# An attention block gated by a mish MLP: products of y in pairs, activations in half places, another order, sums of y in the tail

## The chip, the cores and the metric

The kernel runs on one core of one Trainium2 chip. The metric is device time in microseconds of one execution. Three runs of the kernel before took 3404.28, 3404.55 and 3408.29 us, the median is 3404.55 us.

## The reference

The input x has 2048 rows of 1024 columns, all in float32. There are 32 heads of 32 columns, and the MLP has 3584 hidden columns.

```python
xn = _layernorm(x)
qkv = xn @ wqkv                                   # 1024 -> 3 * 1024
scores = einsum("bhqd,bhkd->bhqk", q, k) * 32 ** -0.5
o = einsum("bhqk,bhkd->bhqd", softmax(scores), v)
s = o @ wo
h = xn @ w1 + b1                                  # 1024 -> 3584
act = h * tanh(softplus(h))                       # mish
g = silu(act @ w2)                                # 3584 -> 1024
out = x + s * g
```

## The kernel before, in words

**Numbers.** Every float32 factor is split in a high part of type fp32r and a low part (what the high part leaves), and a product is three products of such parts (`THREE`). The high parts are mostly copied by ScalarE (`copy`, L276), the low parts are made by VectorE or GpSimd (POOL) as original minus high (`low`, L284). Every matmul writes up to 512 columns into one of eight PSUM banks.

**Stages.** Rows are cut in 16 tiles of 128 and in four chunks of 512. First x is loaded, normalised and turned by TensorE tile by tile, beside the first pass of v (`ln_a` ... `ln_c`, `v_group`, L325); four blocks of W1 are split meanwhile (`w1_first`). Then come two more passes of v, and the projection to q and k (L725), each with splits of further weights in its shadow.

Then comes the planned stage, with five streams of matmuls: s (scores with rows on partitions, only for the maximum of each row, L803; VectorE takes the maxima, L809), t (scores again, transposed, with the maximum subtracted in the product, L890; ScalarE makes p = exp from them, L273), h (hidden columns of the MLP, L1049), y (activations by w2, L1190) and, last, op (the output projection of the first chunk, L1317). The p tiles (2048 columns, six places) are multiplied by v (pv, narrow matmuls, L938) in groups of four, and added to z by POOL (L919) for the sum of the softmax, which a narrow product with ones takes at the end of a head (zp, L974). VectorE adds the pv of a head to o (L950).

**y by seven products.** w2 is multiplied with Strassen's seven products instead of eight. A unit is two hidden blocks of 128 (56 units: 14 in each of the four chunks). `mish` makes four activations of a unit, x, y, z and w, as high and low; x, y and z have 512 columns and w 256; `YSEQ` names the seven products. For each unit and product TensorE makes two sums of three matmuls, each in a bank of its own, and VectorE subtracts each from one of 14 accumulators `yacc` (L1213); the first unit of a chunk is copied by ScalarE. When a chunk is through, seven sums on POOL (`y_sums`, L1226) combine the seven products, and four blocks of 512 KB are stored to `ys`.

**Who sets the order.** The class `Plan` works out, while the program is built, when each engine would be free, and writes the instructions in that order: an operation (`Op`) has an engine, a duration, operations that it needs, and places that it takes and gives in rings: `b` (the eight banks, all), `s`, `t` and `d` (at most so many of the banks for s, for t, and for h and y), `p` (p tiles), `act` and `aw` (activations), `w1`, `w2`. A matmul of a stream has a due time: t by its tile of p, s by the same less `LEAD` tiles, h and y by their unit, y with offsets `Y0` and `Y1`. `run` takes the engine that is free first, gives it the ready operation with the lowest key, and looks again. For VectorE the key is the time at which an operation was ready, less its `urgent` value (`U_MX` for the maxima, `U_Y` for the adds of y).

**q and k of a head** lie in `qstack` and `kstack` (three of each); a head's kstack is free again after the last t of the head, and then holds the head three further on (`stack_load`).

**The tail** (`new_o` to the end) multiplies chunks 1 to 3 of o by wo. Each chunk's eight parts of o are loaded, split into `ohl` or `xo` by `split_o`, and 24 matmuls make half of one of the 16 tiles of the output. `start` loads x and y of a tile, ScalarE takes Silu of y, and `end` multiplies (L1420), adds x (L1421) and stores (L1425). Six places hold x and six y.

Of the kernel before, what the change touches and what calls it, by code (L numbers as in the profile page):

```python
# [26 lines left out]
W1_0, W1_V = 4, 21  # L27
# [7 lines left out]
GROUPS = (4, 4, 4, 4)  # L35

LEAD, LATE = 14, 3.0

PS, ACTS, W1S, W2S, Y0, Y1 = 6, 4, 3, 3, 1.2, 0.14
# [6 lines left out]
S_B, T_B, D_B = 3, 2, 5  # L46

U_MX, U_Y = -3.0, 4.0
# [24 lines left out]
class Op:  # L73


    def __init__(self, eng, took, need=(), emit=None, take=(), give=(), key=None, col=False, late=0.0,
                 bytes_=0, then=None, first=False, both=False, urgent=0.0):
        self.eng, self.took, self.need, self.emit = eng, took, need, emit
        self.take, self.give, self.key, self.col, self.late = take, give, key, col, late
        self.bytes, self.then, self.first, self.both, self.urgent = bytes_, then, first, both, urgent  # L80
        self.end = None


class Plan:
# [94 lines left out]
    def run(self, streams):  # L179
        self.streams = [[s, None] for s in streams]  # L180
        while True:
# [5 lines left out]
            for e in sorted(left, key=self.at.get):  # L187
                now, best, soon = self.at[e], None, None
# [26 lines left out]
                later = [self.at[x] for x in left if self.at[x] > now] + ([soon] if soon is not None else [])  # L215
                if later:
                    self.at[e] = min(later)
                    break
            else:
                raise AssertionError("nothing can go on")  # L220
# [3 lines left out]
def body(ctx: ExitStack, tc: tile.TileContext, x, wqk, wv, wo, w1, b1, w2, out):  # L224
# [21 lines left out]
    ys = [dram.tile([P, 4, D], F32, name=f"ys{i}") for i in range(NC)]  # L246
# [113 lines left out]
    def x_load(t):  # L360
        xt = vp.tile([P, D], F32, tag="x", name=f"x{t}", bufs=5)
        nc.sync.dma_start(xt, x[t * P:(t + 1) * P, :])
# [4 lines left out]
    def split_w(w, raw, job=False):  # L367
        for half in range(2):
# [5 lines left out]
    def w1_first(n, step):  # L374
        t, g = xc[2 + n // 2], n % 2
        raw = first_w1[n // 2][:, g]
        w = t[:, 1, 4 * g:4 * g + 4].rearrange("p k n -> p (k n)") \
# [3 lines left out]
        elif step == 1:  # L381
            split_w(w, raw, True)
# [25 lines left out]
    def ln_b(t):  # L408
        mv, var, rs = stat.pop(t)
        tmps[t] = tmp = vp.tile([P, 1], F32, tag="tmp", name=f"tmp{t}", bufs=3)  # L410
        nc.vector.scalar_tensor_tensor(tmp, rs, var, rs, op0=ALU.mult, op1=ALU.mult)
# [5 lines left out]
    def ln_x(t):  # L417
        tmp, rs = tmps.pop(t)
        act(xts[t], xts[t], AF.Identity, bias=tmp, scale=rs)
# [40 lines left out]
    for t in range(2, NT + 2):  # L460
# [17 lines left out]
        for step, n in enumerate((t - 2, t - 3, t - 5)):  # L478
            if 0 <= n < W1_0:
# [293 lines left out]
    for name, n in (("b", 8), ("s", S_B), ("t", T_B), ("d", D_B), ("o", 1), ("p", PS), ("z", 1), ("e", 1), ("n", 1), ("r", 1), ("on", 1),  # L773
                    ("act", ACTS), ("aw", 1), ("g", 1), ("w1", W1S), ("w2", W2S), ("xc", 1), ("v", 1), ("mx", 2), ("nm", 2), ("hl", 2),
# [101 lines left out]
    def t_stream():  # L876
        pts = {}
        for T in range(NS):
# [29 lines left out]
            if kt:  # L908
# [20 lines left out]
    def product(T, pts, size):  # L929
# [23 lines left out]
        if kt == NT - 1:  # L953

            need.append(adds[T])
# [5 lines left out]
        if kt == NT - 1:  # L961
            norm(h, got[h], adds[T])
# [3 lines left out]
    def norm(h, product_, sum_):  # L966
# [4 lines left out]
        def z_mm(at):  # L971
            t["z"] = bank(at, f"zp{h}")
            for c in range(4):
                nc.tensor.matmul(t["z"][c * DH:(c + 1) * DH, :], ones, zs[h][:, c * 512:(c + 1) * 512],  # L974
                                 start=True, stop=True)
# [23 lines left out]
        a = own = op("PE", 1.0, need=[sum_], emit=z_mm, take=["d", "b"], give=["z"], col=True, late=LATE)  # L999
# [19 lines left out]
    def w2_op(m, need=()):  # L1019
        def emit(at):  # L1020
            w2t[m] = mlp.tile([P, 2, 512], F32R, tag=f"w2{at['w2']}", name=f"w2_{m}")
            move(w2t[m], w2s[m // 7 % U][:, m % 7])
# [40 lines left out]
    def mish(n, made, t):  # L1063
# [9 lines left out]
        def a2(at):  # L1073
            t["q"] = t["h"]
# [5 lines left out]
        def a3(at):  # L1080
            t["r"] = mlp.tile([P, 512], F32, tag="r0", name=f"r{n}")
            act(t["r"], t["q"], AF.Ln, bias=one)

        def d3(at):
            t["n"] = mlp.tile([P, 512], F32, tag="n0", name=f"n{n}")
            nc.vector.scalar_tensor_tensor(t["n"], t["e"], 2.0, t["h"], op0=ALU.add, op1=ALU.mult)

        def a4(at):
            act(t["r"], t["r"], AF.Exp, scale=-1.0)

        def d4(at):
            nc.vector.scalar_tensor_tensor(t["q"], t["q"], 1.0, t["r"], op0=ALU.add, op1=ALU.mult)

        def d5(at):
            nc.vector.scalar_tensor_tensor(t["q"], t["q"], 2.0, t["r"], op0=ALU.subtract, op1=ALU.mult)

        def d6(at):
            nc.vector.tensor_tensor(t["h"], t["h"], t["n"], ALU.mult)

        def hi(kind, r, src):  # L1100
            def emit(at):
                ring = "aw" if kind == "w" else "act"
                if (n // 2, kind) not in acts:
                    w = 256 if kind == "w" else 512
                    acts[n // 2, kind] = mlp.tile([P, 2, w], F32R, tag=f"{ring}{at[ring]}", name=f"a{kind}{n // 2}")
                copy(acts[n // 2, kind][:, 0, r], src()[:, r])
            return emit

        def lo(kind, r, src, eng=None):
            def emit(at):  # L1110
                a = acts[n // 2, kind]
                low(eng or nc.vector, a[:, 1, r], src()[:, r], a[:, 0, r])
            return emit

        L, R, LR = slice(0, 256), slice(256, 512), slice(0, 512)
# [23 lines left out]
        o3 = op("DVE", 0.69, need=[o2], emit=d3, take=["n"])  # L1139
        p2 = op("ACT", 0.69, need=[o3], emit=a2, give=["e"])  # L1140
        p3 = op("ACT", 0.68, need=[p2], emit=a3, take=["r"])
# [3 lines left out]
        o6 = op("DVE", 0.69, need=[o5], emit=d6, give=["n"])  # L1145
# [354 lines left out]
```

## Time and profile before

| what | us |
|---|---|
| median of three runs | 3404.55 |
| the profiled execution's own time | 3404.78 |
| its span, first to last instruction | 3403.0 |
| x, first pass of v | 0 to 83 |
| passes two and three of v | 83 to 213.5 |
| q and k | 213.5 to 583 |
| planned stage | 583 to 3199.4 |
| its end: last y, op of chunk 0 | 3199.4 to 3273 |
| tail: op of chunks 1 to 3 | 3273 to 3403 |

Engines are PE (TensorE's matmuls), PEld (its weight loads, which run beside them), DVE (VectorE), ACT (ScalarE), POOL (GpSimd) and SP (which issues nearly all transfers). A group's row gives line, engine, operation, output and inputs by the program's names, sizes and count, then the busy time and the mean of one in ns, then the idle time ahead of it and what ended it. A row of waits says who waited for whom: total, count and longest. The chain goes back from the last instruction to what released each step.

### The profile page before, as it was taken

The numbers are of one execution on the slowest core, as the hardware profiler recorded it, in microseconds if no ns is written. First come the engines' busy times: TensorE is split into PE (matmuls) and PEld (weight loads), VectorE is DVE, ScalarE is ACT, GpSimd is POOL, SyncE is SP. The second block draws the span as 40 slices with busy tenths as digits, with TensorE's granted clock in tenths as the row PEclk, the third lists the DMA queues.
The fourth block names the chain that finished last, engine by engine and source line by source line (L and its number), as shares of the span: only waits on it lengthen the run. The fifth ranks groups of instructions, "written<-read, shape, count | busy, mean of one in ns | idle before, by whom it ended". The sixth has DMA issues, their size and how long they took to land.

```text
span 3403.0 us, 48050 instructions
## 1 busy us (share of the span) xinstructions
PE 3350.0 (98%) x17107; PEld 2444.7 (72%) x17107; DVE 2683.6 (79%) x4462; ACT 2039.2 (60%) x3394; POOL 2727.3 (80%) x923
## 2 busy tenths in 40 slices
PE   8999999999999999999999999999999999999999
PEld 8898887767766766667777676666776666677587
DVE  6024446999999998889999988889999889896753
ACT  6112222766766667767776677667776776677621
POOL 3547662998898989999989899989988999899910
PEclk9999999999999999999999999999999999999999
DMA  8989997544555465545455564445556555546582
GB/s 285 339 307 370 369 367 243 143 137 138 154 150 148 144 192 180 149 131 153 141 157 157 182 186 137 140 141 148 149 164 198 163 149 158 150 146 193 171 306 85
DMA packets 257633, 639.87 MB, mean 188 GB/s; under 512 B 90266, under 2 KB 99482, under 8 KB 248730
## 3 DMA queue, kind: packets, MB, share of 16 engines
q1 hardware_dynamic: 254948, 628.42, 58.7%
q10 hardware_dynamic: 2448, 8.39, 0.6%
q8 instruction: 136, 2.23, 0.3%
q14 instruction: 101, 0.83, 0.1%
HBM read 474.97 MB, written 160.69 MB: 187 GB/s over the span
## 4 chain that ended last, share of the span: by engine, by line
PE 84%; DVE 7%; DMA 3%; POOL 2%; issue 2%; ACT 1%; SPq 1%; ACTq 0%; DVEq 0%; POOLq 0%
PE h L1049 16%; PE y L1190 13%; PE pv L938 13%; PE s L803 12%; PE t L890 12%; PE qk L725 8%; PE op L1317 4%; PE v L325 4%; DVE mx L809 2%; DMA kstack<-ks 1%; POOL z L919 1%; DVE yacc L1213 1%; ACT p L273 1%; PE zp L974 1%; POOL pw L284 1%
## 5 line engine op out<-in xcount | busy, mean ns | idle before, releaser
L919 POOL TENSOR_TENSOR z<-z,p 128x2048 f32<-128x2048 f32 x448 | 2066.5, 4613 | 75.0 <-ACT p L273 50.6
L273 ACT ACTIVATE p<-t,zero 128x512 f32<-128x512 f32 x2048 | 1366.5, 689 | 455.8 <-PE t L890 436.0
L809 DVE TENSOR_REDUCE mx<-s 128x1 f32<-128x512 f32 x1984 | 1283.4, 682 | 65.9 <-PE s L803 63.4
L890 PE MATMUL t<-qstack,kstack 128*128 128x512 f32 x2048 | 791.3, 394 | 1.8 <-ACT p L273 0.9
L803 PE MATMUL s<-kstack,qstack 128*128 128x512 f32 x1984 | 755.6, 397 | 14.8 <-DMA kstack<-ks 7.5
L1049 PE MATMUL h<-xr,w 128*128 128x512 f32 x2016 | 676.6, 390 | 1.4 <-DVE aw L284 0.6
L1213 DVE TENSOR_TENSOR yacc<-yacc,y 128x512 f32<-128x512 f32 x728 | 492.6, 680 | 36.8 <-PE y L1190 33.3
L803 PEld LDWEIGHTS s<-kstack,qstack 128*128 128x128 f32 x1984 | 366.8, 188 | 160.8 <-issue 26.8
L890 PEld LDWEIGHTS t<-qstack,kstack 128*128 128x128 f32 x2048 | 382.0, 188 | 126.5 <-issue 28.5
L938 PE MATMUL pv<-p,v 128*32 128x512 f32 x4096 | 466.0, 595 | 1.0 <-ACT p L273 0.6
L1049 PEld LDWEIGHTS h<-xr,w 128*128 128x128 f32 x2016 | 377.6, 188 | 84.1 <-DVE aw L284 2.1
L725 PE MATMUL qk<-xc,qkw 128*128 128x512 f32 x1536 | 351.3, 389 | 0.3
L725 PEld LDWEIGHTS qk<-xc,qkw 128*128 128x128 f32 x1536 | 288.0, 188 | 60.8 <-DVE mx L607 1.2
L938 PEld LDWEIGHTS pv<-p,v 128*32 128x32 f32 x4096 | 119.9, 109 | 276.4 <-issue 247.6
L919 POOL TENSOR_TENSOR z<-p,p 128x2048 f32<-128x2048 f32 x32 | 147.8, 4620 | 159.5 <-PE zp L974 107.1
L1190 PE MATMUL y<-w,az 128*128 128x512 f32 x672 | 232.1, 395 | 4.7 <-POOL az L284 1.7
L1190 PE MATMUL y<-w,ay 128*128 128x512 f32 x672 | 227.2, 391 | 3.4 <-ACT ay L276 1.4
L1190 PE MATMUL y<-w,ax 128*128 128x512 f32 x672 | 225.1, 391 | 2.2 <-DVE ax L284 0.7
L1049 PE MATMUL h<-xc,w 128*128 128x512 f32 x672 | 225.7, 391 | 0.0
L950 DVE TENSOR_TENSOR o<-o,pv 128x512 f32<-128x512 f32 x96 | 65.9, 687 | 117.0 <-PE pv L938 112.9
L1190 PEld LDWEIGHTS y<-w,az 128*128 128x128 f32 x672 | 125.1, 189 | 37.1 <-DVE yacc L1213 3.1
L1190 PEld LDWEIGHTS y<-w,ay 128*128 128x128 f32 x672 | 125.2, 188 | 33.2 <-DVE yacc L1213 3.5
(134 smaller groups left out, 3627.8 us busy)
## 6 DMA issues: line engine op xcount, KB each, us to landing
w<-w2s SPq DMA_DIRECT2D x392, 512.0 KB
w<-w1s SPq DMA_DIRECT2D x224, 512.0 KB
w2s<-pw SPq DMA_DIRECT2D x98, 512.0 KB
qstack<-qs SPq DMA_DIRECT2D x96, 256.0 KB
kstack<-ks SPq DMA_DIRECT2D x96, 256.0 KB
w1s<-w1h SPq DMA_DIRECT2D x34, 512.0 KB
x<-in_A_x_dram SPq DMA_DIRECT2D x32, 512.0 KB
qs<-qst SPq DMA_DIRECT2D x32, 512.0 KB
```

Of the source, the lines that this page charges most:

```text
L273: nc.scalar.activation(out_, in_, fn, bias=zero if bias is None else bias, scale=scale)
L325: nc.tensor.matmul(ps[:, :cols], xc[t // 4][:, a, k, (t % 4) * P:(t % 4 + 1) * P], w(b, k), start=n == 0, stop=n == 3 * KT - 1)
L725: nc.tensor.matmul(ps, w[:, k // 4, a, k % 4], xc[c][:, b, k], start=n == 0, stop=n == 3 * KT - 1)
L803: nc.tensor.matmul(sp_, qst[h % 3][:, qt * P:(qt + 1) * P], kst[h % 3][:, kc * 512:(kc + 1) * 512], start=True, stop=True)
L809: nc.vector.reduce_max(tiles["mx"][:, qt, kc:kc + 1], tiles[qt, kc], axis=AX.X)
L890: nc.tensor.matmul(tp, kst[h % 3][:, kt * P:(kt + 1) * P], qst[h % 3][:, c * 512:(c + 1) * 512], start=True, stop=True)
L919: nc.gpsimd.tensor_tensor(zs[h], pts[T - 1] if kt == 1 else zs[h], pts[T], ALU.add)
L938: nc.tensor.matmul(t["b"][c * DH:(c + 1) * DH, :], vt[h][:, k, :], pts[T - kt + k][:, c * 512:(c + 1) * 512], start=k == kt - size + 1, st ...
L1049: nc.tensor.matmul(t["h"], w1t[m_][:, a, k % 4], xts_[c][:, b, k], start=i == 0, stop=i == 3 * KT - 1)
L1190: nc.tensor.matmul(t["y"], acts[B, kind][:, p, half * 256 + s * P:half * 256 + (s + 1) * P], w2t[m_][:, q], start=i == 0, stop=i == 2)
L1213: nc.vector.tensor_tensor(ya, ya, t["y"], ALU.subtract)
L1317: nc.tensor.matmul(ps[t, dh], ohl[t // 4, k][:, a, s * P:(s + 1) * P], wt[k][b][:, r], start=k == 0 and i == 0, stop=k == KT - 1 and i == 2)
```

## The change

1. **y in pairs.** Two units (even and odd B) share the banks of a product: six matmuls of the one unit and six of the next end in the same two banks, and one add to `yacc` serves both. There are 336 adds on VectorE instead of 728, and the same 56 copies of ScalarE. w2's blocks are loaded in the new order.
2. **Half places.** Activations lie in places of 256 columns (x, y and z in two, w in one; `act` has ten, `aw` goes). High and low of x and y are made in two halves each, and so are the lows of z on POOL.
3. **mish with two tiles.** The squares no longer lie in h's bank but in an SBUF tile (`r0`); Square stands right behind the first Exp; tile `n0` goes.
4. **The scheduler** looks at all engines that are idle at the earliest time before time moves on.
5. **Numbers:** `LEAD` 14 to 8, `LATE` 3 to 4, `S_B` 3 to 2, `U_MX` -3 to 1, `U_Y` 4 to 1, other offsets for y.
6. **The last head's last two p tiles** (`ZP = 2`) are no longer added by POOL; TensorE adds them in the product with ones (eight matmuls more), and the last pv doesn't wait for z.
7. **Sums of y:** only chunk 0 is summed in the plan. For chunks 1 to 3 the seven accumulators are stored as they are (`y_store`), loaded in the tail in seven blocks (`y_load`, pool `yp`), and summed there on POOL (`y_total`). Silu takes a tile in two halves. x has five places in the tail.
8. **The start:** tile 0 of x is loaded and normalised in halves; three blocks of W1 instead of four are split in the first pass, later and in halves; the small steps of the normalisation (`ln_b`) go to POOL from tile 2 on.

```diff
-W1_0, W1_V = 4, 21
+W1_0, W1_V = 3, 21
-LEAD, LATE = 14, 3.0
+LEAD, LATE = 8, 4.0
-PS, ACTS, W1S, W2S, Y0, Y1 = 6, 4, 3, 3, 1.2, 0.14
+PS, ACTS, W1S, W2S, Y0, Y1, Y2 = 6, 10, 3, 3, 0.6, 0.4, 0.6
+ORDER = [(0, 0), (0, 1), (1, 0), (1, 1)]
-S_B, T_B, D_B = 3, 2, 5
-U_MX, U_Y = -3.0, 4.0
+S_B, T_B, D_B = 2, 2, 5
+U_MX, U_Y = 1.0, 1.0
...
-            for e in sorted(left, key=self.at.get):
-                now, best, soon = self.at[e], None, None
+            now = min(self.at[e] for e in left)
+            idle, soon = [], None
+            for e in left:
+                if self.at[e] > now:
+                    continue
+                best = None
...
-        for step, n in enumerate((t - 2, t - 3, t - 5)):
-            if 0 <= n < W1_0:
+        if t - 2 < W1_0:
+            w1_first(t - 2, 0)
+        for step in (3, 1, 2):
+            n, odd = divmod(t - 4 - step, 2)
+            if not odd and 0 <= n < W1_0:
                 w1_first(n, step)
...
-            if kt:
+            if kt and T < NS - ZP:
                 add(T, pts)
...
+            terms = [zs[h]] + ([pts[i] for i in range(NS - ZP, NS)] if h == H - 1 else [])
+            for i, p in enumerate(terms):
+                for c in range(4):
+                    nc.tensor.matmul(t["z"][c * DH:(c + 1) * DH, :], ones, p[:, c * 512:(c + 1) * 512],
+                                     start=i == 0, stop=i == len(terms) - 1)
...
+        def part(u, kind, half, src, need, eng="DVE", give=()):
+            high = made_by[u, kind, half] = op("ACT", 0.4, need=need, emit=hi(kind, half, src), take=["act"])
+            eng_ = nc.gpsimd if eng == "POOL" else nc.vector
+            act_ops[u, kind, half] = op(eng, 0.62 if eng == "POOL" else 0.45, need=[high], emit=lo(kind, half, src, eng_),
+                                        give=give, key=-1 if eng == "POOL" else None)
...
-        for B in range(NC * U):
+        for B in range(0, NC * U, 2):
...
+                        first, last = v == 0 and i == 0, v == 1 and i == 2
...
-            if b == U - 1:
-                free = y_sums(c, done)
+            while c == NC - 1 and b == U - 2 and H - 1 not in stored:
+                yield None
+            if b == U - 2:
+                free = (y_store if c else y_sums)(c, done)
...
+    def y_total(c):
+        for i, j in ((4, 0), (0, 2), (1, 4), (4, 5), (4, 6), (3, 1), (5, 1)):
+            nc.gpsimd.tensor_tensor(yt[c, i], yt[c, i], yt[c, j], ALU.add)
...
             if t + 4 < NT:
                 start(t + 4)
+            if c + 1 < NC and s < 2:
+                y_load(c + 1, ((4, 0, 2, 1), (5, 6, 3))[s])
+            if c + 1 < NC and s == 2:
+                y_total(c + 1)
```

The order shows what this does to the engines. First TensorE's row where the last head's p tiles are multiplied, near the end of the plan; `pv31_15` is the last product of head 31, `zp31` its sum, `y54_1_0` the first bank of product 1 for the pair of units 54 and 55 (before, `y55_5_0` is of unit 55 alone), `op0_0` the first part of the output projection. Before:

```order
L1317 MATMUL op0_0_32202<-wo0_30669,xo0_32170 128x512 x2
L1190 MATMUL y55_5_0_32219<-w2_390_32180,az55_32156 128x512 x2
L938 MATMUL pv31_15_32224<-p508_31985,v31_31570 32x512 x4
L938 MATMUL pv31_15_32224<-p509_32032,v31_31570 32x512 x4
L938 MATMUL pv31_15_32224<-p510_32071,v31_31570 32x512 x4
L938 MATMUL pv31_15_32224<-p511_32112,v31_31570 32x512 x4
L974 MATMUL zp31_32243<-z31_31577,ones_145 32x512 x4
L1190 MATMUL y55_5_0_32219<-w2_390_32180,az55_32156 128x512
L1190 MATMUL y55_5_1_32256<-w2_390_32180,az55_32156 128x512 x3
```

After:

```order
L910 MATMUL t511_3_31660<-qstack1_5009,kstack1_5010 128x512
L1217 MATMUL y54_1_1_31668<-w2_380_31609,ax1_54_31256 128x512 x3
L1217 MATMUL y54_1_0_31653<-w2_381_31632,ax1_55_31602 128x512 x3
L958 MATMUL pv31_15_31686<-p508_31510,v31_31095 32x512 x4
L958 MATMUL pv31_15_31686<-p509_31556,v31_31095 32x512 x4
L958 MATMUL pv31_15_31686<-p510_31607,v31_31095 32x512 x4
L958 MATMUL pv31_15_31686<-p511_31639,v31_31095 32x512 x4
L996 MATMUL zp31_31719<-z31_31099,ones_145 32x512 x4
L996 MATMUL zp31_31719<-p510_31607,ones_145 32x512 x4
L996 MATMUL zp31_31719<-p511_31639,ones_145 32x512 x4
L1217 MATMUL y54_1_1_31668<-w2_381_31632,ax1_55_31602 128x512 x3
```

The last product of the head has moved from behind most of the last unit's products to right behind the last t, ahead of five of the last pair's seven products.

Second, ScalarE's row in the tail, where the last parts of chunk 1's o are copied (`ohl1_6`, `ohl1_7`) and Silu of tile 4 is taken (`y3_4` before; `yp1_0` and `yp1_4`, two blocks of chunk 1's sums, after). Before:

```order
L276 ACTIVATE ohl1_5_32537<-oraw1_5_32538 128x512
L1425 DMA out_0_dram<-x3_2_32554 128x1024
L276 ACTIVATE ohl1_6_32540<-oraw1_6_32541 128x512
L273 ACTIVATE y3_4_32573<-y3_4_32573,zero_143 128x1024
L276 ACTIVATE ohl1_7_32543<-oraw1_7_32544 128x512
L1425 DMA out_0_dram<-x3_3_32558 128x1024
```

After:

```order
L282 ACTIVATE ohl1_5_32120<-oraw1_5_32121 128x512
L1482 DMA out_0_dram<-x3_2_32141 128x1024
L282 ACTIVATE ohl1_6_32123<-oraw1_6_32124 128x512
L279 ACTIVATE yp1_0_32159<-yp1_0_32159,zero_143 128x512
L279 ACTIVATE yp1_4_32157<-yp1_4_32157,zero_143 128x512
L282 ACTIVATE ohl1_7_32126<-oraw1_7_32127 128x512
```

POOL makes these blocks, with rows that were not there before:

```order
L1465 TENSOR_TENSOR yp1_4_32157<-yp1_4_32157,yp1_0_32159 128x1024
L1465 TENSOR_TENSOR yp1_0_32159<-yp1_0_32159,yp1_2_32161 128x1024
L1465 TENSOR_TENSOR yp1_1_32163<-yp1_1_32163,yp1_4_32157 128x1024
L1465 TENSOR_TENSOR yp1_4_32157<-yp1_4_32157,yp1_5_32174 128x1024
L1465 TENSOR_TENSOR yp1_4_32157<-yp1_4_32157,yp1_6_32176 128x1024
```

Where tile 4's Silu took a loaded y, it now takes the result of five sums on POOL, and it stands ahead of the copy of `ohl1_7` as before.

More of the change, by code (lines that the diff above doesn't have):

```diff
@@ L214, in run @@
                     break
[L215 to L216 removed]
+                idle.append(e)
+            else:
+                later = [self.at[e] for e in left if self.at[e] > now] + ([soon] if soon is not None else [])
+                assert later
+                for e in idle:
                     self.at[e] = min(later)
[L218 to L220 removed]
 @with_exitstack
@@ new lines, in y_stream @@
+                        m = Op("PE", MM, key=tile_time * due, emit=mm, need=[act_ops[B + v, kind, half], w2_ops[m_]],
+                               take=["d", "b"] if first else [], give=give)
+                        if first:
+                            t["own", s] = m
+                        yield m
+                        if "w2" in give and W2S + (at_ := freed[0]) < NC * U * 7:
+                            w2_op(W2S + at_)
+                        freed[0] += "w2" in give
+                        if not last:
+                            continue
@@ L1428, in body @@
         new_o(1, k)
-    for t in range(4):
-        start(t)
-    act(yt[0], yt[0], AF.Silu)
+    start(0)
+    y_load(0, (0, 4))
+    start(1)
+    y_load(0, (3, 5))
+    start(2)
+    start(3)
+    silu(0)
     for k in range(4):
@@ L1443, in body @@
                 if dh == 0 and t + 1 < NT:
[L1444 removed]
+                    silu(t + 1)
                 if c:
```

226 lines of the change are left out of this document (120 added, 106 removed).

## The prediction

> **What bounds the kernel now.** I began with the page (engine shares, the chain that ended last by engine), then took the windows by stage, the chain in order of time, the matmul groups of the planned stage, and last the waits ahead of them.
>
> ```profile
> PE 3350.0 (98%) x17107; PEld 2444.7 (72%) x17107; DVE 2683.6 (79%) x4462; ACT 2039.2 (60%) x3394; POOL 2727.3 (80%) x923
> ...
> PE 84%; DVE 7%; DMA 3%; POOL 2%; issue 2%; ACT 1%; SPq 1%; ACTq 0%; DVEq 0%; POOLq 0%
> ```
>
> TensorE is busy for 98% of the span and carries 84% of the chain. But records of matmuls overlap, so "busy" hides short waits; I need the pace of a matmul that waits for nothing. The chain gives it for a wide matmul (1,128 in a row) and for a pv product of four p tiles (32 narrow matmuls); its last rows are a load and the run of the tail.
>
> ```profile
> 213.62 255.72 PE qk L725 x1128
> ...
> 601.49 3.57 PE pv L938 x32
> ...
> 3247.12 7.30 DMA y<-ys
> 3272.81 125.67 PE op L1317 x553
> ```
>
> That is 255.72/1128 = 0.2267 us a wide matmul. Next the windows of the planned stage and of its end (length, then busy time and count of PE, PEld, VectorE, ScalarE and POOL, clock, DMA share, rate), and of the first the groups of narrow and small matmuls:
>
> ```profile
> 583.00:3199.40 2616.40, 2593.30 (x13380) 1809.39 (x13380) 2336.22 (x3922) 1839.77 (x3043) 2365.93 (x642) 1.00 0.53 156
> 3199.40:3273.00 73.60, 65.36 (x290) 47.89 (x289) 55.55 (x57) 25.25 (x35) 42.20 (x14) 0.98 0.75 263
> ```
>
> ```profile
> L938 PE MATMUL pv<-p,v 128*32 128x512 f32 x4064 | 462.3, 595 | 1.0 <-ACT p L273 0.6 <-DVE yacc L1213 0.2
> ...
> L974 PE MATMUL zp<-z,ones 128*32 128x512 f32 x248 | 32.3, 592 | 0.0
> L580 PE MATMUL mtp<-ident_r,hl 128*128 128x128 f32 x32 | 8.4, 264 | 0.3 <-ACT p L273 0.3
> ```
>
> Of 13,380 matmuls 4,064 + 248 + 32 are these, so 9,036 are wide (s, t, h, y): x 0.2267 = 2048.5 us. The pv products are 4064/32 = 127, at 3.57 us 453 us; the 248 of z, of the same size, 248/32 x 3.57 = 28 us. So 2530 of 2616.4 us is work, and about 86 us is loss: waits, switches between wide and narrow, and the 32 little transposes. Only this loss, the start, the end of the plan and the tail can be won, because the number of matmuls does not fall. Who causes the loss:
>
> ```profile
> PEld s L803 <- DVE mx L809: 23.4, 46, 2.4
> PEld s L803 <- DVE o L950: 15.4, 19, 0.8
> PEld y L1190 <- DVE yacc L1213: 11.8, 25, 1.0
> ...
> PEld t L890 <- ACT p L273: 10.9, 34, 1.1
> ...
> PE s L803 <- DMA kstack<-ks: 7.5, 7, 2.0
> ```
>
> A row reads: who waits, for whom, sum, count, longest. Those of PEld are idle times of the weight load, which runs ahead of the matmul, so they are upper bounds. The clearest message is that TensorE waits for VectorE to empty banks.
>
> **The change, part by part.** *y in pairs, sums in the tail, half places (VectorE).* The load of VectorE in the middle, and the groups that change:
>
> ```profile
> 1200.00:1800.00 600.00, 594.15 (x3058) 413.02 (x3058) 538.31 (x908) 420.32 (x695) 547.62 (x150) 1.00 0.53 156
> ```
>
> ```profile
> L1213 DVE TENSOR_TENSOR yacc<-yacc,y 128x512 f32<-128x512 f32 x728 | 492.6, 680 | 36.8 <-PE y L1190 33.3
> ...
> L284 DVE TENSOR_TENSOR aw<-h,aw 128x256 fp32r<-128x256 f32 x55 | 22.9, 417 | 0.7 <-ACT aw L276 0.5
> ```
>
> VectorE is at 538.31/600 = 0.90. Two units in a bank leave 336 adds of 728: 392 x 0.680 = 266.6 us go. The lows of x and y were 112 of 512 columns (taken at the add's 0.680: 76 us) and become 224 of 256 (0.417: 93 us): 17 us come. Net 250 us of 2616, so the load falls from 0.90 to 0.80. ScalarE makes 224 copies for 112; even at 0.417 each with the old ones free this adds 93 us in 2616, and 420.32/600 = 0.70 becomes 0.74 at most: hidden behind TensorE, as nothing in the rows above waits long for ScalarE but t. The price if that cover were gone is the 93 us less what the old copies took.
>
> For the wait at a server with such loads I use load/(1 - load) as an estimate: 9 at 0.90, 4 at 0.80, so waits fall by about half. The bounds 23.4, 15.4 and 11.8 overstate; I take half of each as real. Waits of s for the max: half of 11.7, -6. Waits of s for o's adds: half of 7.7, -4. Waits of y for its add: half as many bank groups, each half the wait, 5.9 x 3/4 = -4.5. Smaller ones of h and pv of this kind I take together at another -4. Bounds of the four: 59 gained (the 86 less 7.5 of kstack, 10.9 of t and 8.4 of the small transposes), and +10, where the waits move: a y bank now stands open over about 8 us of TensorE's order instead of 1.1 us, and h and y share five banks.
>
> The nine more stores of 512 KB lie under TensorE at a DMA share of 0.53 (the window's next to last column). Mish's new order (Square right behind Exp, two tiles for three) changes no count; it lies on ScalarE, 0.26 idle, and if that cover went each of the 112 chains would end later, none would cost more.
>
> *Two s banks for three, nearer s (LEAD 14 to 8).* Counted in the order, the TensorE work between an s and the s that needs its bank has a median of 2.95 us before and 2.04 us after; a max reads a bank as the add does, and I take its 0.68 us, so a wait needs VectorE to be over 1.3 us late. This eats part of the gain above (it is why I don't take more), and it is a rival below. LEAD is in p tiles, of 2616/512 = 5.1 us: kstack is freed by a head's last t, and the next reader was due two tiles later (16 - 14), now eight. The 7 waits of up to 2.0 us say that some loads take 10 + 2 us; eight tiles are 41 us, so all of it goes: -7.5 (bounds -7.5, 0).
>
> *Sums of y off the plan (POOL).*
>
> ```profile
> L1226 POOL TENSOR_TENSOR yacc<-yacc 128x1024 f32<-128x1024 f32 x21 | 50.1, 2403 | 0.4
> ```
>
> Of 21 sums in the plan seven stay: 14 x 2.4 = 34 us off POOL, which holds the p tiles by its z adds; halves of az give some 10 us back. Through "t waits for p" (at most 10.9) I take -3 (bounds -10.9, +5). The scheduler's rule by itself has no row; its worth lies in the order that the other terms use. The planned stage sums to -6 - 4 - 4.5 - 4 - 7.5 - 3 = -29; bounds -77 and +15.
>
> *The last head (ZP = 2).* Sixteen narrow matmuls less eight that were there add eight pairs, half a pv product: +1.8. They free the last pv from two z adds.
>
> *The end of the plan.*
>
> ```profile
> 3208.37 0.72 PE L1190 MATMUL y<-w,az 128*128 128x512 f32 x2 [1.40 <-DMA w<-w2s]
> 3210.77 1.89 PE L1190 MATMUL y<-w,az 128*128 128x512 f32 x4 [1.68 <-POOL az L284]
> ...
> 3224.76 1.45 PE L1317 MATMUL op<-wo,xo 128*128 128x512 f32 x5 [1.84 <-DVE wo L284]
> ```
>
> Three waits, 4.9 us, and four matmuls in 1.89 us where 4 x 0.2267 = 0.9 would do. The new order has pv and the sums of z before most of the last y pair, and op pieces between; -4 (bounds -8, +4: a pair needs both units' tiles, so az may be late in its turn).
>
> *The start.*
>
> ```profile
> 58.78 1.03 PE L426 MATMUL pt<-ident,x 128*128 128x128 f32 x8
> ...
> 64.15 1.65 PE L325 MATMUL v<-vw,xc 128*128 128x256 f32 x6 [2.19 <-DVE xc L284]
> 65.60 1.89 PE L426 MATMUL pt<-ident,x 128*128 128x128 f32 x8
> ```
>
> A late x load stops TensorE for 2.19 us, and the same eight transposes then take 1.89 instead of 1.03 us. The 1 MB writes of w1s that stood ahead of that load on SP go out later, so both go: -3; halving x0's load and its normalising is worth about half a normalising of 1.2 us: -1. Against it, six small POOL operations for four of VectorE, in a queue with splits of W1. Sum -4 (bounds -7, +2). On the clock, the Trainium skill (TensorE: Matmul & The Clock Gate, section "What's actually happening") says that half speed comes after an idle window of about 3.4 us. The trace disagrees here: a stop of 2.19 us was enough. By that rule alone the 0.86 us would not come back, and the start would be worth 0.9 less.
>
> *The tail.* ScalarE's row now has Silu of tile 4 ahead of the last copy of chunk 1's ohl; this Silu waits for POOL's sums, these for yp loads, and the last three of those stand on SP behind x_5, which waits for tile 0's store.
>
> ```profile
> 3213.30 8.08 DVE L284 TENSOR_TENSOR xo<-or,xo 128x512 fp32r<-128x512 f32 x3
> ...
> 3256.21 2.50 DVE L284 TENSOR_TENSOR ohl<-oraw,ohl 128x512 fp32r<-128x512 f32 x4 [13.30 <-ACT ohl L276]
> ```
>
> ```profile
> 3261.39 0.37 ACTq L1425 DMA_DIRECT2D out_dram<-x  x1
> ```
>
> Tile 0's store left at 3261.39, 11.4 us ahead of chunk 1's long run of matmuls (3272.81). The load of x_5 must wait for this store, and the yp loads follow: I take them together at little over the 7.30 us of a y load, 9 us; then three sums of 2.4 (7.2), then Silu, copy and low, about 3. That is 19 us, so ohl1_7 is ready near 3280.4; its first reader is the 22nd matmul, 4.8 us into the run: 3277.6. A stop of about 3 us, some 1 us of slow clock behind it as in the start, and VectorE beside POOL is slow: the rows show 8.08/3 = 2.7 us for lows beside POOL's sums and splits, and 2.50/4 = 0.63 for the same lows without. Taken together +6 (bounds 0, +16). The Trainium skill (GPSIMD Engine Reference, section "8. Key points") says that GpSimd shares SBUF interfaces with VectorE, in contention with VectorE instructions with two SBUF inputs. The trace agrees (2.7 against 0.63 us), and it speaks against moving sums beside these lows.
>
> **Sum.** The profiled execution took 3404.78 us, 0.2 above the median of 3404.55. -29 + 1.8 - 4 - 4 + 6 = -29.2, which gives 3375.6; I say 3375 us. All low bounds together would be -90, all high ones +39, and neither comes about at once.
>
> **Rivals.** *Only the sure parts.* VectorE's lighter load does not shorten the waits, since the order is drawn anew to run closer and two s banks use up what was freed. The four terms of it (18.5) drop out and the rest stays: 3375.6 + 18.5 = 3394. For it: the waits for the max are 23.4/46 = 0.5 us each, less than one operation, and this does not shrink with load. Against: the load falls by 0.1.
>
> *The tail stops longer.* If the yp loads land as late as others in a crowd and VectorE's lows each wait for a sum, the stop is 15 us rather than 3: +12, 3387. For it: the rows above. Against: SP has less to load then.
>
> *Slower: two s banks.* VectorE often has two operations in front of a max: 3 x 0.68 = 2.05 us is the median distance to the next use of the bank. If one of the 1,984 s in ten waits 0.35 us, half an operation, 198 x 0.35 = 69 us, and the time is 3375 + 69 = 3444. It decides from 29/0.35 = 83 such waits on, one s in 24. Against: the order is drawn with the banks counted in, at a duration of 0.69 for the max.
>
> **How the numbers follow.** Forecast 0.55 (3354 to 3392), only sure parts 0.20, tail 0.15, two s banks 0.10. A measurement of this kernel can tell about 0.2%, 6.8 us: 3397.7 and 3411.4. The sure-parts case ends above 3397.7 in about a third, the tail in a few of a hundred; so faster 0.82, same 0.08, slower 0.10. For 8 in 10: low 3340 (beyond it, one in twenty), high 3402 (beyond it, the slow rival and a part of the sure one).
>
> **What would show it.** Right: VectorE near 0.80 in the middle; 336 adds; waits of s for kstack gone and for the max about halved; planned stage near 2587 us; 64 us without a 2 us stop. Wrong: s waits for mx of over 23 us; a hole of over 10 us before chunk 1's matmuls; or a planned stage as long as before with new waits behind az or p.

## The result, and the profile after

The changed kernel takes 3377.96 us (median of five runs, 3376.62 to 3378.30) against 3404.57 us of the kernel before on the same chip: a ratio of 0.9918, 95% interval 0.9907 to 0.9930. The forecast was 3375 us. The profiled execution took 3378.12 us, its span is 3376.3 us, 26.7 below the span before.

The page of the changed kernel, first the engines' shares, then the group of adds of y:

```profile
PE 3334.9 (99%) x17123; PEld 2454.0 (73%) x17123; DVE 2505.0 (74%) x4126; ACT 2059.6 (61%) x3523; POOL 2741.2 (81%) x1061
...
L1243 DVE TENSOR_TENSOR yacc<-yacc,y 128x512 f32<-128x512 f32 x336 | 228.4, 680 | 34.4 <-PE y L1217 33.5
```

The 336 adds are there, at 680 ns each as before. How full the middle is shows a stretch of equal length in both. First before, then after (length, then busy time and count of PE, PEld, VectorE, ScalarE, POOL, clock, DMA share, rate):

```profile
700.00:3100.00 2400.00, 2377.49 (x12277) 1655.59 (x12276) 2161.00 (x3633) 1673.57 (x2763) 2173.82 (x591) 1.00 0.53 156
```

```profile
700.00:3100.00 2400.00, 2398.86 (x12516) 1693.98 (x12518) 2030.79 (x3431) 1735.13 (x2942) 2200.62 (x644) 1.00 0.54 160
```

In 2400 us TensorE now issues 239 matmuls more, and its idle time falls from 22.5 to 1.1 us. VectorE's load goes from 0.900 to 0.846. The waits of s in the planned stage of the changed kernel:

```profile
PEld s L823 <- DVE o L970: 7.7, 10, 0.8
...
PEld s L823 <- DVE mx L829: 3.4, 11, 0.5
```

The weight loads of s waited 23.4 us for maxima before, and 3.4 now; for o's adds 15.4, and 7.7 now; for the load of kstack there is no row any more. These rows and the 336 adds are among the signs that the prediction named for being right; another of its signs, VectorE near 0.80 in the middle, is not there.

Not all got shorter. The start of the planned stage, TensorE's timeline:

```profile
582.00 0.77 PE L910 MATMUL t<-qstack,kstack 128*128 128x512 f32 x1 [2.74 <-DMA qstack<-mt]
...
664.40 0.39 PE L1076 MATMUL h<-xc,w 128*128 128x512 f32 x1
668.00 1.19 PE L1217 MATMUL y<-w,ay 128*128 128x512 f32 x2 [3.21 <-DMA w<-w2s]
...
669.97 5.40 PE L958 MATMUL pv<-p,v 128*32 128x512 f32 x32
```

The stop of 3.21 us, for a block of w2, is new. That of 2.74 us, for the maxima on their way into qstack, takes the place of a shorter one that the kernel before has there:

```profile
582.21 0.78 PE L803 MATMUL s<-kstack,qstack 128*128 128x512 f32 x2 [1.83 <-DVE mx L607]
```

Behind the stop of 3.21 us a pv product takes 5.40 us instead of 3.57: the granted clock is 0.50 from 666.75 to 673.57 us. SP's timeline ahead of it:

```profile
642.24 8.48 SPq L286 DMA_DIRECT2D w<-w1s  x2
651.31 0.32 SPq L286 DMA_DIRECT2D w<-w2s  x1
...
657.06 0.37 SPq L286 DMA_DIRECT2D w<-w2s  x1
```

SP stands 8.48 us at two loads of W1, and between the two blocks of w2 it issues a head's q and k.

The end of the plan, in TensorE's timeline:

```profile
3160.13 1.90 PE L996 MATMUL zp<-p,ones 128*32 128x512 f32 x16
...
3170.15 0.96 PE L1357 MATMUL op<-wo,xo 128*128 128x512 f32 x3 [3.34 <-DVE xo L290]
...
3194.70 1.84 PE L1217 MATMUL y<-w,aw 128*128 128x512 f32 x6 [2.30 <-DMA w<-w2s]
```

The 16 narrow matmuls added for z (sixteen, where the list of the change says eight: TensorE's count goes from 17107 to 17123) take 1.90 us; op waits for its own activations and the last y for w2. Then TensorE ahead of chunk 1's run, and the window around it:

```profile
3230.45 4.24 PE L1357 MATMUL op<-wo,ohl 128*128 128x512 f32 x18
3237.12 1.22 PE L1357 MATMUL op<-wo,ohl 128*128 128x512 f32 x2 [2.43 <-ACT ohl L282]
3238.85 1.95 PE L1357 MATMUL op<-wo,ohl 128*128 128x512 f32 x3 [0.50 <-DVE ohl L290]
3244.36 2.08 PE L1357 MATMUL op<-wo,ohl 128*128 128x512 f32 x4 [3.57 <-DVE ohl L290]
```

```profile
3196.00:3244.40 48.40, 41.90 (x170) 32.87 (x168) 26.92 (x25) 12.14 (x19) 18.52 (x7) 0.89 0.92 348
```

Here is the hole in the tail: 2.43 + 0.50 + 3.57 = 6.5 us idle. The clock is 0.89 over these 48.4 us, and what it takes is 3.8 us, the rest of the 10.3 us that the table below gives for this stretch. Of these 3.8 us some 1.7 do not belong to the hole: the clock is at 0.50 from 3196.02 to 3199.43 us, behind the stop of 2.30 us for w2.

To place the 26.7 us I worked out TensorE's loss from the trace: for each matmul its start minus the start of the one before, minus the pace (0.227 us; 0.318 into a narrow product, 0.522 out of one), summed where it is over 3 ns. Slow clock counts as loss.

| stage | loss before | loss after | change | forecast |
|---|---|---|---|---|
| to the first qk (its start, 213.5 and 210.6) | | | -2.9 | -4 |
| q and k | 2.9 | 3.7 | +0.8 | 0 |
| planned stage to 700 us | 5.2 | 13.4 | +8.2 | |
| 700 us to shortly before the last t | 70.9 | 25.0 | -45.9 | -29 with the row above |
| from there to the last y | 9.7 | 11.0 | +1.3 | -4 |
| last y to chunk 1's run (fill) | 3.6 | 10.3 | +6.7 | +6 with the next row |
| chunk 1's run to the end | 0.1 | 1.5 | +1.4 | |
| narrow matmuls added to zp (1.90 us above) | | | +1.9 | +1.8 |
| sum | | | -28.5 | -29.2 |

The sum misses the span by 1.8 us, which I don't place.

### The profile page after: what moved, and what is told of

It reads as the page before. It is cut to its first block, busy times and chain, and to the rows that moved or that the text cites. A ratio compares the mean times of both kernels' runs of the same rounds, so it can differ in the third digit from the quotient of the medians.

```text
span 3376.3 us, 47946 instructions
## 1 busy us (share of the span) xinstructions
PE 3334.9 (99%) x17123; PEld 2454.0 (73%) x17123; DVE 2505.0 (74%) x4126; ACT 2059.6 (61%) x3523; POOL 2741.2 (81%) x1061
## 5 line engine op out<-in xcount | busy, mean ns | idle before, releaser
L939 POOL TENSOR_TENSOR z<-z,p 128x2048 f32<-128x2048 f32 x446 | 2057.3, 4613 | 70.9 <-ACT p L279 46.7
L829 DVE TENSOR_REDUCE mx<-s 128x1 f32<-128x512 f32 x1984 | 1317.1, 685 | 181.2 <-PE s L823 176.0
L823 PE MATMUL s<-kstack,qstack 128*128 128x512 f32 x1984 | 775.3, 394 | 0.7 <-DMA w<-w1s 0.4
L1076 PE MATMUL h<-xr,w 128*128 128x512 f32 x2016 | 729.3, 390 | 0.1
L823 PEld LDWEIGHTS s<-kstack,qstack 128*128 128x128 f32 x1984 | 371.7, 188 | 111.9 <-issue 13.4
L1217 PE MATMUL y<-w,ay 128*128 128x512 f32 x672 | 250.6, 394 | 3.5 <-DMA w<-w2s 3.2
L1243 DVE TENSOR_TENSOR yacc<-yacc,y 128x512 f32<-128x512 f32 x336 | 228.4, 680 | 34.4 <-PE y L1217 33.5
L1217 PE MATMUL y<-w,az 128*128 128x512 f32 x672 | 250.4, 390 | 0.0
L1076 PE MATMUL h<-xc,w 128*128 128x512 f32 x672 | 247.3, 391 | 0.0
L1217 PE MATMUL y<-w,ax 128*128 128x512 f32 x672 | 246.0, 391 | 1.2 <-DMA w<-w2s 0.8
L1217 PEld LDWEIGHTS y<-w,ax 128*128 128x128 f32 x672 | 125.9, 188 | 31.7 <-issue 2.5
L1076 PEld LDWEIGHTS h<-xc,w 128*128 128x128 f32 x672 | 126.6, 189 | 26.6 <-DVE mx L627 0.2
```

The source lines that it names most:

```text
L823: nc.tensor.matmul(sp_, qst[h % 3][:, qt * P:(qt + 1) * P], kst[h % 3][:, kc * 512:(kc + 1) * 512], start=True, stop=True)
L829: nc.vector.reduce_max(tiles["mx"][:, qt, kc:kc + 1], tiles[qt, kc], axis=AX.X)
L939: nc.gpsimd.tensor_tensor(zs[h], pts[T - 1] if kt == 1 else zs[h], pts[T], ALU.add)
L1076: nc.tensor.matmul(t["h"], w1t[m_][:, a, k % 4], xts_[c][:, b, k], start=i == 0, stop=i == 3 * KT - 1)
L1217: nc.tensor.matmul(t["y", s], acts[A, kind, half][:, p, s * P:(s + 1) * P], w2t[m_][:, q], start=first, stop=last)
L1243: nc.vector.tensor_tensor(ya, ya, t["y", s], ALU.subtract)
```

## Experiments

Theory: the middle's gain comes from VectorE (fewer adds of y, so less load and shorter waits for banks) and from kstack loaded earlier; the tail's loss from POOL's sums. Rivals: the scheduler's rule or the urgencies did it; two banks for s cost something that is hidden; fewer hand-overs of banks did it, whatever the load. Each edit also makes `Plan` draw the whole order anew; e6, e7 and e12 below, which change the rule alone, move the time by some 6, 2 and 1 us, so a difference of that size tells little of its cause. All times are medians; the kernel before took 3404.5 to 3405.8 us beside them. "Middle" is the loss of the fourth row of the table, 25.0 in the changed kernel and 70.9 before; "load" is VectorE's busy share from 700 to 3100 us.

**e1, y unpaired.** Each unit has its own banks and adds; the order of the matmuls stays a pair's.

```diff
-                        first, last = v == 0 and i == 0, v == 1 and i == 2
+                        first, last = i == 0, i == 2
...
-                        done[j, s] = op("DVE" if b else "ACT", 0.69 if b else 0.6, emit=y_add, urgent=U_Y,
+                        done[j, s] = op("DVE" if b + v else "ACT", 0.69 if b + v else 0.6, emit=y_add, urgent=U_Y,
...
```

> The changed kernel (3378.0 us), but each unit's sum of a product in a bank of its own again: 392 more adds of y on VectorE, and bank groups half as long; half places, scheduler, numbers, start and tail stay changed. Theory (the load of VectorE: with 0.90 of its time taken TensorE waits for banks, with 0.85 hardly): most of the 45.7 us that TensorE no longer loses between 700 us and the last t come back, so 3410 to 3425 us, and waits of s for the maxima return to some 20 us. Rival (the new scheduler rule and the numbers gave the gain, the load of VectorE did not matter): 3376 to 3386 us.

3388.56 us, ratio to before 0.9954 (0.9939 to 0.9969): 10.6 us above the changed kernel, between both expectations. The window:

```profile
700.00:3100.00 2400.00, 2393.95 (x12446) 1679.37 (x12444) 2194.92 (x3774) 1712.71 (x2919) 2186.80 (x641) 1.00 0.54 159
```

VectorE's load is 2194.92/2400 = 0.915, higher than before the change (0.900), yet the middle loses 40.6 us and not 70.9. The theory that the load alone sets the waits falls here; a third of the middle's gain (15.6 of 45.9) comes back. The weight loads of s wait 5.9 us for maxima, not the 20 that were expected. e1 also doubles the hand-overs of y's banks; how the 15.6 us divide between these and the load stays open.

**e2 and e5, load added.** After each of the 336 adds VectorE takes a maximum over the accumulator that nobody reads. In e2 its result is a new tile of 4 bytes in the pool `mlp`; in e5, whose edit is shown, it is written to `pad`, which was there.

```diff
+                        if b:
+                            op("DVE", 0.69, need=[done[j, s]], urgent=U_Y,
+                               emit=lambda at, j=j, s=s: nc.vector.reduce_max(pad[:, 0:1], yacc[:, j, s], axis=AX.X))
```

> The changed kernel, with a maximum over an accumulator in SBUF (no use of its result, about 0.68 us) after each of the 336 adds of y on VectorE: VectorE's load goes back up by some 229 us of 2600, while the banks and the matmuls keep their pairs. Theory (load): at least half of the 45.7 us comes back, 3400 to 3420 us, with waits of s for the maxima above 15 us. Rival (the gain comes from longer bank groups, that is from half as many hand-overs of a bank between TensorE and VectorE, whatever the load): 3376 to 3386 us.

> As the run before with a maximum after each of the 336 adds on VectorE, but the result is written to a tile that exists already, so that no place in SBUF shifts. In that run wide matmuls came every 0.2317 us through the planned stage instead of every 0.2274, some 37 of its 61 us, and a new tile of 4 bytes had shifted the places. Theory (the shift made matmuls slower, and the added load of 229 us costs the rest): 3390 to 3405 us at a pace of 0.2275. Rival (VectorE's load itself slows the matmuls, or all of the 61 us): 3430 to 3440 us. Third (load costs nothing): 3376 to 3382 us.

e2 took 3439.14 us (1.0105, 1.0088 to 1.0122), above both expectations, e5 3404.84 us (0.9999, 0.9990 to 1.0009). The stretch of e2, then that of e5:

```profile
700.00:3100.00 2400.00, 2386.57 (x12218) 1650.87 (x12217) 2156.63 (x3674) 1681.30 (x2859) 2145.29 (x626) 1.00 0.52 155
```

```profile
700.00:3100.00 2400.00, 2385.41 (x12376) 1675.74 (x12375) 2169.53 (x3709) 1705.31 (x2907) 2176.32 (x636) 1.00 0.53 158
```

PE is as busy in both, but e2 gets 158 matmuls less done: a wide matmul comes every 0.2317 us in e2 and every 0.2275 in e5 (mean distance of two starts, those over 0.3 us left out). The place of that result, and with it the shift of the places made after it, is the only difference of the two programs, whose instructions stand in the same order on every engine, so 34 us of e2 are the shift's. e5 says that 336 operations more cost 26.9 us, over twice as much as e1's 392 adds, and its middle loses 51.4 us at a load of 0.904, below e1's 0.915. So operations on VectorE do cost TensorE time, with the banks still in pairs, but how much does not follow the load. Rows of e5 and of e1, in this order:

```profile
PEld s L823 <- DVE mx L829: 13.2, 27, 1.2
```

```profile
PEld s L823 <- DVE mx L829: 5.9, 18, 0.7
```

In e5 the weight loads of s wait longer for maxima. Why its operations cost more than e1's is not shown: they do not come in bursts behind the adds, since only 30 of the 336 follow an add directly and 190 follow a maximum.

**e3, LEAD 14.**

```diff
-LEAD, LATE = 8, 4.0
+LEAD, LATE = 14, 4.0
```

> The changed kernel with LEAD 14 instead of 8: s runs six p tiles further ahead. Theory (a head's kstack was loaded too late): waits of s for the load of kstack come back, 5 to 10 us in the sum, 3383 to 3390 us. Rival (those loads were late because VectorE and the rest ran late, and are on time in the changed order anyway): 3375 to 3381 us, with no such waits.

3390.09 us (0.9963, 0.9948 to 0.9978), 12.1 above, a little over the expected 5 to 10. The waits for kstack are back, the row is that of e3:

```profile
PE s L823 <- DMA kstack<-ks: 8.7, 5, 2.4
```

The middle loses 44.0 us, 19 more: kstack's own 8.7 and as much again that LEAD moves elsewhere.

**e4, three banks for s.**

```diff
-S_B, T_B, D_B = 2, 2, 5
+S_B, T_B, D_B = 3, 2, 5
```

> The changed kernel with three banks for s instead of two. Theory (with the lighter VectorE two banks cost nothing): 3374 to 3382 us. Rival (two banks make TensorE wait for maxima, hidden in other waits): faster by 8 us or more, 3370 us or less.

3378.08 us (0.9921, 0.9907 to 0.9936): no difference. Two banks cost nothing here.

**e6 and e7, the scheduler's rule.** e6 puts the old `run` into the changed kernel, e7 the new one into the kernel before.

```diff
-            now = min(self.at[e] for e in left)
-            idle, soon = [], None
-            for e in left:
-                if self.at[e] > now:
-                    continue
+            for e in sorted(left, key=self.at.get):
+                now, best, soon = self.at[e], None, None
...
```

> The changed kernel with the scheduler's old rule (the engine that is free first, then look again). Theory (the rule gives a good part of the 30 us in the middle that unpairing y did not give back): 3388 to 3408 us. Rival (the rule only shuffles): 3374 to 3382 us.

> The kernel before with the scheduler's new rule as its only change. Theory (the rule is worth 10 to 30 us): 3375 to 3395 us. Rival (only shuffles): 3398 to 3410 us.

e6 took 3372.25 us (0.9904, 0.9889 to 0.9919), 5.7 less than with the new rule and below both expectations; e7 3408.09 us (1.0007, 0.9998 to 1.0016). The rule is no source of the gain. e6's middle (27.2) is no better; it loses 3.3 us less between the last t and the last y (its traced run took 3376.40 us, the slowest of its four).

**e8, chunk 1's sums back in the plan.**

```diff
-                free = (y_store if c else y_sums)(c, done)
+                free = (y_store if c > 1 else y_sums)(c, done)
...
-                y_load(c + 1, ((4, 0, 2, 1), (5, 6, 3))[s])
-            if c + 1 < NC and s == 2:
+                y_load(c + 1, ((4, 0), (5, 3))[s] if c == 0 else ((4, 0, 2, 1), (5, 6, 3))[s])
+            if 0 < c < NC - 1 and s == 2:
                 y_total(c + 1)
```

> The changed kernel with the seven sums of chunk 1 back in the plan (chunks 2 and 3 stay in the tail), so that POOL is idle while the last parts of chunk 1's o are split. Theory (the hole ahead of chunk 1's long run, 2.4 + 0.5 + 3.6 us idle and as much slow clock, comes from POOL's sums and from Silu waiting for them): 3364 to 3373 us, the hole below 1.5 us. Rival (the seven sums, 17 us of POOL, hold up the sums of z in the plan and cost as much): 3374 to 3382 us.

3364.22 us (0.9879, 0.9864 to 0.9894), 13.7 below the changed kernel. What stood in the way is seen in VectorE's timelines ahead of chunk 1's run, first of the changed kernel, with POOL's sums beside it, then of e8:

```profile
3225.05 2.42 DVE L290 TENSOR_TENSOR ohl<-oraw,ohl 128x512 fp32r<-128x512 f32 x1 [1.08 <-ACT ohl L282]
3227.40 0.68 DVE L1477 TENSOR_TENSOR yp<-op,yp 128x512 f32<-128x512 f32 x1
3228.11 2.17 DVE L1478 TENSOR_TENSOR x<-x,yp 128x512 f32<-128x512 f32 x1
3230.20 2.88 DVE L290 TENSOR_TENSOR ohl<-oraw,ohl 128x512 fp32r<-128x512 f32 x1
```

```profile
3224.51 8.02 POOL L1465 TENSOR_TENSOR yp<-yp,yp 128x1024 f32<-128x1024 f32 x3 [54.97 <-DMA yp<-ys]
3233.10 10.66 POOL L1465 TENSOR_TENSOR yp<-yp,yp 128x1024 f32<-128x1024 f32 x4 [0.57 <-DMA yp<-ys]
```

```profile
3220.78 0.69 DVE L290 TENSOR_TENSOR ohl<-oraw,ohl 128x512 fp32r<-128x512 f32 x1 [1.08 <-ACT ohl L282]
3221.39 0.68 DVE L1477 TENSOR_TENSOR yp<-op,yp 128x512 f32<-128x512 f32 x1
3222.11 0.69 DVE L1478 TENSOR_TENSOR x<-x,yp 128x512 f32<-128x512 f32 x1
```

Beside POOL's sums the lows and the adds of x, which read two operands in SBUF, take 1.7 to 2.9 us (seven of them from 3225 to 3244 us) instead of 0.69; the product with a bank as one operand (L1477) takes 0.68 in both. ScalarE then stands behind such an add, since it issues the store of the output in its row:

```profile
3236.05 0.34 ACTq L1482 DMA_DIRECT2D out_dram<-x  x1
3236.44 0.63 ACT L282 ACTIVATE ohl<-oraw 128x512 fp32r<-128x512 f32 x1 [9.67 <-DVE x L1478]
...
3238.28 0.72 ACT L279 ACTIVATE yp<-yp,zero 128x512 f32<-128x512 f32 x1 [0.59 <-POOL yp L1465]
```

The copy of ohl waits 9.67 us for the add of x; Silu waits only 0.59 us for POOL. In e8 the fill and the run lose 1.3 us together instead of 11.8, and the middle is no worse (24.7) with seven more sums in it. That is 10.5 of the 13.7 us. e8 also loads four blocks for chunk 1 in the tail instead of seven, but transfers are as dense in its fill, while POOL (the last count in brackets) rests:

```profile
3191.40:3230.80 39.40, 39.40 (x170) 32.47 (x169) 16.22 (x26) 12.03 (x19) 0.00 (x0) 0.97 0.93 349
```

**e9, unpaired and LEAD 14 together** (the diffs of e1 and e3).

> The changed kernel with both undone: each unit's sum of y in a bank of its own (alone 3388.6 us, 10.6 above the changed kernel) and LEAD 14 (alone 3390.1, 12.1 above). Theory (two causes side by side, VectorE's adds and kstack loaded late): the costs add up, 3396 to 3406 us. Rival (both fill the same waits, so the second costs little): 3388 to 3394 us.

3391.64 us (0.9960, 0.9947 to 0.9973), 13.7 above the changed kernel and not 22.7. The rival holds: the two fill the same waits. The middle loses 46.4 us; 24.5 of the 70.9 are still accounted for by neither, more than half of its gain.

**e10, old urgencies.**

```diff
-U_MX, U_Y = 1.0, 1.0
+U_MX, U_Y = -3.0, 4.0
```

> The changed kernel with the old urgencies on VectorE (maxima -3, adds of y 4, instead of 1 and 1). Theory (with two banks for s the maxima must come early; these two numbers hold most of the 11 us of the middle that pairs and LEAD leave open): 3384 to 3395 us, with more waits of s for the maxima. Rival (the planner orders VectorE well by either): 3374 to 3382 us.

3385.93 us (0.9946, 0.9930 to 0.9961), 8.0 above, with the middle at 40.7. The row of e10 that grew most:

```profile
PEld s L823 <- DVE o L970: 16.9, 21, 0.8
```

It was 7.7 in the changed kernel; that for maxima rose from 3.4 to 7.9. At a load of 0.844, about the same as after the change, the order alone costs 15.7 us of the middle. The whole time's 8.0 us are not far above what a new order can do by itself.

**e11 and e12, on from e8.** e11 puts the sums of chunk 2 into the plan too, e12 gives e8 the old rule.

```diff
-                free = (y_store if c > 1 else y_sums)(c, done)
+                free = (y_store if c > 2 else y_sums)(c, done)
...
```

> The changed kernel with the sums of chunks 1 and 2 in the plan, only those of chunk 3 in the tail. Theory (only the sums that run beside the fill cost; those of chunk 2 run beside 48 us of matmuls of chunk 1 that nothing else stops): no different from chunk 1's alone, 3361 to 3367 us. Rival (each set of sums in the tail costs): 3358 us or less. Other rival (seven more sums in the plan hold up the sums of z): 3368 us or more.

> The changed kernel with the sums of chunk 1 in the plan (alone 3364.2 us) and the scheduler's old rule (alone 3372.3 us, 5.7 below the changed kernel). Theory (both gains are real and lie in different places): 3356 to 3361 us. Rival (the old rule's gain was a shuffle of the end of the plan, which this end does not repeat): 3362 to 3367 us.

e11 took 3362.53 us (0.9878, 0.9862 to 0.9893), not to be told from e8: only the sums beside the fill cost. Its middle loses some 5 us more than e8's, which its end of the plan and its fill win back. e12 took 3365.51 us (0.9886, 0.9868 to 0.9904): the old rule's 5.7 us do not come again, so they were a shuffle. e8 and e11 are faster than both kernels.

## Why the prediction was right, step by step

- **The size and the main cause held.** -29.2 was forecast, -26.7 came in the spans. That TensorE's waits for VectorE and kstack in the planned stage would go was the forecast's main step, and the rows of waits and e1, e3 and e5 show it. That the size came out so near is in part luck: by the table the planned stage up to the last t gave 8.7 us more than forecast (-45.9 + 8.2 against -29), and the other stages together 9.4 us less.
- **The step from load to waits did not hold as it was put.** It took load/(1 - load), from 0.90 to 0.80. The load fell only to 0.846. The durations of VectorE's instructions in the planned stage do add up to 243 us less (2624 before, 2381 after; 250 were reckoned), but its busy time, in which instructions that overlap count once, fell by 178 (2340 and 2162): the prediction took mean durations from a busy time. And the waits do not follow the load: 40.6 us lost at 0.915 (e1), 51.4 at 0.904 (e5), 70.9 at 0.900 (before), 40.7 at 0.844 (e10), 25.0 at 0.846. The order in VectorE's row counts too, as e10 shows; that it is what stands ahead of an urgent instruction is the likely reading, not a shown one. The four terms for VectorE's waits were put at 18.5 us, and e1 gives back 15.6 of the middle; but the middle gave 45.9 us where 29 was forecast for the whole planned stage.
- **kstack was mis-sized**: 7.5 forecast, 12.1 by e3, which holds all that LEAD moves; that a late load throws off what follows it is argued. It is not additive with the pairs (e9).
- **The urgencies were left out.** They were named in the change and not priced; e10 puts them at 8.0 us alone (15.7 in the middle). How the 24.5 us that e9 leaves divide among the urgencies, the half places, mish's order and the due times of y stays open; the last three were not tried one by one.
- **The start of the planned stage was not foreseen**: +8.2 us, a stop of 2.74 us where 1.83 stood before, a new one of 3.21 us, and slow clock behind both (before, behind the one). That the block of w2 was issued behind the load of a head's q and k and a wait for a place of w1 is what SP's timeline shows; no run took that away, so it is argued, not shown.
- **The end of the plan** was forecast at -4 and came at +1.3: new stops for blocks of w2 (2.30 us) and for xo (3.34 us) took the place of the old ones.
- **The tail** was forecast at +6 and came at +8.1, and e8 shows the sums as the cause of nearly all of it. Of the two mechanisms the lesser was put first: Silu's wait for POOL is 0.59 us, VectorE's slowing beside POOL carries the hole.
- **POOL's sums off the plan** were put at -3; e8 and e11 put 7 and 14 sums back into the plan with no loss in the whole time, so the term is nothing that these runs can tell.
- **The start** gave 2.9 of 4. TensorE's timeline of the changed kernel, at the place of the stop of before:

```profile
62.79 0.98 PE L331 MATMUL v<-vw,xc 128*128 128x256 f32 x6 [1.47 <-DVE xc L290]
63.61 1.03 PE L443 MATMUL pt<-ident,x 128*128 128x128 f32 x8
```

The stop is 1.47 us instead of 2.19, and not gone; the eight transposes behind it take 1.03 us again.

The rivals: "only the sure parts" falls by its time and with the rows of waits, though its doubt that the lighter load by itself shortens them is borne out by e10; "two s banks" falls with e4; "the tail stops longer" lay at +18 against a measured +8.1.

## What to carry to other kernels

Where one engine empties the banks of another, the engine's load is not enough to price an edit; look at the order of its row too. Here 336 operations cost 27 us in e5 and 392 cost 11 in e1, at nearly the same load, and two numbers of urgency cost 15.7 us of the middle at an unchanged one. Work that is moved off a full stage needs a place where its side effects hurt nobody; chunk 1's sums on POOL slowed VectorE about threefold where TensorE had no slack, and the same sums a stage earlier were free. An edit that ends late loads can be worth more than the waits that name them: 12.1 us here for a row of 8.7.

## What the runs showed of the hardware

- **Places in SBUF set the matmul's pace.** One more tile of 4 bytes, and with it the shift of the tiles placed after it, made the wide matmuls of the planned stage come every 0.2317 us in the mean instead of 0.2275 (e2 against e5), with nothing else changed: 34 us of 3405. y's products show it most (0.2333 against 0.2276). It is not the running of the added maxima: from 600 to 740 us, ahead of the first of them at 745.9 us, y's products already stand at a median of 0.232 in e2 and 0.227 in e5.
- **The clock falls after short stops, and their length alone does not decide it.** Two places of TensorE's timeline in e10:

```profile
1228.77 0.79 PE L823 MATMUL s<-kstack,qstack 128*128 128x512 f32 x1 [1.37 <-DVE mx L829]
1229.49 4.97 PE L958 MATMUL pv<-p,v 128*32 128x512 f32 x32
...
1885.38 1.15 PE L1217 MATMUL y<-w,ax 128*128 128x512 f32 x4 [3.04 <-DMA w<-w2s]
...
1886.69 3.64 PE L958 MATMUL pv<-p,v 128*32 128x512 f32 x32
```

After 1.37 us (with a stop of 0.45 just ahead) the clock fell to 0.50 and pv took 4.97 us; after 3.04 us it stayed at 1.00 and pv took 3.64. It matters how the stop lies on a fixed raster of time. In the changed kernel's trace the stretches at 0.50 begin at 581.41, 666.75, 3172.13, 3196.02 and 3236.98 us: these lie 25, 734, 7 and 12 steps of 3.413 us apart, and each stretch lasts one to three steps. In the fourteen traces, without the first 20 and last 8 us of each, all 36 steps at full clock in which TensorE stood still for over 1.92 us were followed by a low clock, 19 of the 57 with 1.40 to 1.92 us, and none with less. The two stops of e10 each fill 1.8 us of a step, where the runs went either way. The Trainium skill (TensorE: Matmul & The Clock Gate, section "What's actually happening") puts the fall behind an idle window of about 3.4 us. Here a step of that length that was idle for little more than half was enough, so the measurements decide.
- **POOL slows VectorE by operand.** Beside a sum on POOL an operation of VectorE with two operands in SBUF took 1.7 to 2.9 us for 0.69; one with a bank as an operand was not slowed (0.68). The Trainium skill (GPSIMD Engine Reference, section "8. Key points") names this contention; the factor of two and a half to four is this trace's.
